# Attention and two feed-forward layers on one core: a chunk's last transpose tied to a product with 64 weight columns

## The chip, the cores and the metric

The kernel runs on one NeuronCore of a Trainium2 chip. The metric is the time of one execution on the device in microseconds (us), as a median of several runs. Five engines work side by side, each through its own list of instructions in order: TensorE (PE, matrix products and transposes; its weight loads show as PEld), VectorE (DVE), ScalarE (ACT), GpSimd (POOL) and SyncE (SP, which here only issues transfers). Products write to PSUM, eight banks of 128 x 512 numbers in float32; the other engines read them there.

## The reference

Attention over buckets, 2 batches x 8 heads x 768 tokens x 64 columns, then two feed-forward layers on 1536 tokens of 512 columns:

```python
q_bits = (einsum(q, proj) > 0); k_bits = (einsum(k, proj) > 0)   # 6 bits each
mask = q_bucket[:, :, :, None] == k_bucket[:, :, None, :]
scores = where(mask, q @ k.T / sqrt(64), -1e9)
attn = exp(scores - max); attn = attn / (sum(attn) + 1e-9)
x = (attn @ v)                         # -> 1536 x 512
h = x @ w_in;  x = (h * tanh(log1p(exp(h)))) @ w_out      # first layer, 2048 wide
h = x @ w_in2; x = (h - tanh(h)) @ w_out2                 # second layer
```

## The kernel before, in words

**Precision.** A number is kept as a high part (rounded to the PE's fast float32 form) and a low part (the rest). A product of two such numbers is made from high x high, high x low and low x high.

**Attention** goes through 8 pairs of heads. For a pair `g` each of the two heads `h` has two halves of 384 query tokens. A half takes three score tiles (`scores`, 128 tokens against 768 keys, four products, L507 and L508), into the only buffer `s` of two banks. DVE copies a tile to `p` with an upper clamp and takes its minimum on the way (L511, "clamp" below); ACT makes the exponentials and their sums (L533). The mask is part of the scores: the products in L508 carry the bits of the buckets beside the low parts of q and k. The bits come from a product with the planes (`piece`, L412 to L414, 64 weight columns), written to `z` (L395 on ACT, L397 on DVE), and from there by transfers into the stacks `c` and `d`; for the very first stack they are also written straight into `c` and `d`.

Then the half goes through 6 chunks of 128 keys (`chunk`): three PE transposes of `p` into a bank `pt` (L554), ACT's copy of it to the high part `ph` (L567), DVE's subtraction for the low part `pl` (L570), and a pair of products with the values `vt` (L578 with `ph`, L579 with `pl`). `vt` has 128 columns, 64 high and 64 low, so both products have 128 weight columns, and the output's two halves of 64 rows hold "times high" and "times low"; `gather` adds them into `u` (L586 on ACT, L589 on DVE). In three of a head's twelve chunks ("pooled") ACT copies to `f`, and POOL makes `ph` and `pl` from that (L319, L563). After the second head, `finish` makes the reciprocals of the sums (`rden`, L602 and L607 on DVE), spreads them (`wide`), transposes them on PE (L619) and multiplies (L626).

**Feed-forward.** The weights arrive as 64-bit words and are converted on DVE, ACT and POOL (`convert`, L711 to L740); the products are L756 to L758 and L815. The last block's results are copied to `osb` (two buffers) and sent out by SP (L865, L862).

**The order.** The whole program is first recorded as operations with a cost and a key (`op`). `Plan.order` then plays them through engine by engine with these costs, with the number of buffers and with a delay `LATE` between engines, takes at each step what can start first, and among equals the lowest key; in that order they are issued. Keys count in ticks of 1.16; a product's key lies `PV_LAG` ticks behind its chunk's. So other costs or other groupings change the order on all engines. PE takes its instructions strictly in the order made.

Of the kernel before, what the change touches and what calls it, by code (L numbers as in the profile page):

```python
# [39 lines left out]
N_A = 5  # L40
# [5 lines left out]
TAIL = 3  # L46
WARM = 7


G_BUFS, E_BUFS, GX_BUFS, F_BUFS = 3, 3, 2, 4  # L50
T_BUFS, O_BUFS, P_BUFS, U_BUFS = 3, 2, 6, 3

# [3 lines left out]
SPARE = 1  # L56
LATE = 0.25
LATS = 0.15
# [9 lines left out]
AHEAD = 8  # L68
PV_LAG = 4.0
PIECE = 2.5  # L70
# [4 lines left out]
V_REL = 14.0  # L75
Q_REL = 8.0
OUT_LAG = 13.0
RAW = 12.0
# [150 lines left out]
def tile_lsh_attention_moe(  # L229
# [55 lines left out]
    for name, m0, m1 in (("wb", N_A, N_A + N_B), ("wc", N_A + N_B, KF)):  # L285
        for tag in slots(m0, m1).split():
# [8 lines left out]
        memory("left", (  # L295
            ("const", "", 1), ("xy", "", 1), ("wa", slots(0, N_A), 1), ("osb", "osb", O_BUFS), ("t", "t", T_BUFS),
            ("g", "ph", G_BUFS), ("e", "pl", E_BUFS), ("f", "f", F_BUFS),
# [13 lines left out]

    zero = plan.pools["osb"].tile([P, XB], F32, tag="osb", name="zero")
    hot = plan.pools["osb"].tile([P, XB], F32R, tag="osb", name="hot")

# [86 lines left out]
    def piece(g, nm, half, key):  # L401

        if (g, "z") not in stacks:
            stacks[g, "z"] = buf("z", "z", [64, S], F32R)
        z, (th, tl) = stacks[g, "z"], stacks[g, nm]
        c = slice(half * HB, (half + 1) * HB)
        y = buf("ps_t", "pt", [P, 512])
        r0 = 0 if nm == "k" else 32

        def planes():  # L410
            o = y()[:64, :HB]
            nc.tensor.matmul(o, pjh, th()[:, c], start=True, stop=False)  # L412
# [3 lines left out]
        op("PE", 0.53, key + 0.3, planes, [(th, half), (tl, half)], [y])  # L416
# [123 lines left out]

    def chunk(g, h, half, c, ps, o, key):

# [7 lines left out]

        def transpose():
            for t in range(TB):
                pc = ps[t]().rearrange("p a b -> p (a b)")
                nc.tensor.transpose(pt()[:, t * P:(t + 1) * P], pc[:, c * P:(c + 1) * P], ident)  # L554

        op("PE", 0.41, key, transpose, ps, [pt])
        if pooled:
            pf = buf("f", "f", [P, XB])
            op("ACT", 0.38, key + 0.1, lambda: nc.scalar.copy(pf()[:, w], pt()[:, :HB]), [pt], [pf])
            op("POOL", 0.5, key + 0.2, lambda: pool_copy(ph()[:, w], pf()[:, w]), [pf], [ph], lat=LATG)  # L560
# [5 lines left out]
        else:  # L566
            op("ACT", 0.38, key + 0.1, lambda: nc.scalar.copy(ph()[:, w], pt()[:, :HB]), [pt], [ph])  # L567
            op(
# [3 lines left out]
                ),  # L572
                [pt, ph], [pl],
# [66 lines left out]
    for g in range(len(pairs)):  # L640
# [22 lines left out]
        for h in range(2):  # L663
            for half in range(2):
# [3 lines left out]
                ]  # L668
                o = buf("ps_t", "pt", [P, 512])
                for c in range(NT):  # L670
                    chunk(g, h, half, c, ps, o, at(NT * n + c))
                gather(h, o, us[half], at(NT * (n + 1)) + PV_LAG)
                if h == 1:
                    finish(g, half, us[half], at(NT * (n + 1)) + PV_LAG + 0.3)

# [146 lines left out]
    def feed_forward(which, j, first):  # L822
# [17 lines left out]
        for d, (a, n) in enumerate(acc):  # L840
# [13 lines left out]
            else:  # L854
                b, t = divmod(j * TX + d, NT)
                rows = out[b * S:(b + 1) * S, :].rearrange("(t p) d -> t p d", p=P)[t]
                osb = buf("osb", "osb", [P, DM])
                eng, cost, e = (("ACT", 0.48, nc.scalar.copy), ("DVE", 0.6, nc.vector.tensor_copy))[d % 2]
                if tail and d == KD - 1:
                    for i in range(2):  # L860
                        c = slice(i * hm, (i + 1) * hm)
                        op("ACT", 0.26, key, lambda osb=osb, a=a, n=n, c=c: nc.scalar.copy(osb()[:, c], a()[:, n, c]), [(a, n)], [(osb, i)])  # L862
                        dma(P * hm * 4, key, lambda rows=rows, c=c: rows[:, c], lambda osb=osb, c=c: osb()[:, c], [(osb, i)], [("out", j, d, i)])
                    continue
# [97 lines left out]
```

## Time and profile before

| what | value |
|---|---|
| median of 3 runs | 792.76 us (791.81 to 794.22) |
| profiled execution | 792.33 us, of which the span in the profile 790.6 us |
| PE busy | 769.4 us, 97% of the span |
| DVE, ACT, POOL busy | 489.3, 408.0, 302.1 us |
| attention | about 20 to 250 us |
| granted PE clock, mean | 0.997 |

The profile is of one execution. An idle time with an arrow is time in which the engine had nothing to do, and names what ended it; a PE instruction's length has a modelled end, so the distance between two starts says more than the length. The start of a product right behind a transpose is shown early, by the time that the transpose still takes; the start of the product after that one is true again.

### The profile page before, as it was taken

The numbers are of one execution on the slowest core, as the hardware profiler recorded it, in microseconds if no ns is written. First come the engines' busy times: TensorE is split into PE (matmuls) and PEld (weight loads), VectorE is DVE, ScalarE is ACT, GpSimd is POOL, SyncE is SP. The second block draws the span as 40 slices with busy tenths as digits, with TensorE's granted clock in tenths as the row PEclk, the third lists the DMA queues.
The fourth block names the chain that finished last, engine by engine and source line by source line (L and its number), as shares of the span: only waits on it lengthen the run. The fifth ranks groups of instructions, "written<-read, shape, count | busy, mean of one in ns | idle before, by whom it ended". The sixth has DMA issues, their size and how long they took to land.

```text
span 790.6 us, 10579 instructions
## 1 busy us (share of the span) xinstructions
PE 769.4 (97%) x3799; PEld 647.2 (82%) x3799; DVE 489.3 (62%) x792; ACT 408.0 (52%) x799; POOL 302.1 (38%) x308
## 2 busy tenths in 40 slices
PE   7999999999998899999999999999999999999997
PEld 5799898898887788887888888888887888888886
DVE  7888888898898998862111279889832322232221
ACT  6889899899888455443121345465522222222122
POOL 4676667667658766540000056555500000000000
PEclk9999999999999999999999999999999999999999
DMA  6574474563790460000000354530000100010001
GB/s 168 138 171 110 106 165 107 114 159 85 183 353 20 185 240 1 1 0 1 1 0 27 107 212 167 208 133 1 1 0 1 54 0 1 1 53 1 1 0 54
DMA packets 23009, 65.82 MB, mean 83 GB/s; under 512 B 3494, under 2 KB 4390, under 8 KB 22956
## 3 DMA queue, kind: packets, MB, share of 16 engines
q1 hardware_dynamic: 22524, 64.65, 27.5%
q8 instruction: 30, 0.49, 0.2%
q10 hardware_dynamic: 432, 0.49, 0.2%
q14 instruction: 23, 0.19, 0.1%
HBM read 43.09 MB, written 3.15 MB: 58 GB/s over the span
## 4 chain that ended last, share of the span: by engine, by line
PE 79%; DVE 12%; ACT 5%; issue 2%; DMA 1%; POOL 0%; ACTq 0%; DVEq 0%; POOLq 0%
PE s L815 17%; PE pt L815 16%; PE pt L758 11%; PE pt L756 11%; PE pt L757 11%; DVE p L511 4%; PE s L507 3%; PE pt L554 3%; PE s L508 3%; ACT p L533 2%; DVE pl L570 2%; PE pt L579 2%; PE pt L578 2%; DVE u L589 1%; DVE z L397 1%
## 5 line engine op out<-in xcount | busy, mean ns | idle before, releaser
L758 PE MATMUL pt<-xh,wi 128*128 128x512 f32 x384 | 151.1, 394 | 2.4 <-POOL wi L740 2.4
L756 PE MATMUL pt<-xh,wi 128*128 128x512 f32 x384 | 151.0, 393 | 0.0
L757 PE MATMUL pt<-xl,wi 128*128 128x512 f32 x384 | 150.7, 393 | 0.0
L794 DVE TENSOR_TENSOR pt<-pt,f 128x512 f32<-128x512 f32 x48 | 33.4, 697 | 118.1 <-ACT f L791 118.1
L784 DVE TENSOR_TENSOR pl<-f,ph 128x512 fp32r<-128x512 f32 x48 | 47.7, 996 | 88.3 <-ACT ph L781 88.1
L732 POOL TENSOR_TENSOR t<-t,wi 128x512 uint32<-128x512 uint32 x32 | 48.0, 1499 | 133.8 <-ACT wi L727 128.0
L533 ACT ACTIVATE p<-p,mn 128x768 f32<-128x768 f32 x96 | 90.3, 941 | 15.6 <-DVE p L511 13.3
L511 DVE TENSOR_SCALAR_CACHE_REDUCE p<-s 128x768 f32<-128x768 f32 x93 | 88.2, 948 | 12.7 <-PE s L508 12.0
L780 ACT ACTIVATE f<-pt 128x512 f32<-128x512 f32 x48 | 28.7, 598 | 129.8 <-PE pt L758 129.3
L791 ACT ACTIVATE f<-pt 128x512 f32<-128x512 f32 x48 | 28.7, 598 | 126.9 <-PE pt L758 126.6
L554 PE MATMUL pt<-cst,p 128*128 128x128 f32 x576 | 89.4, 272 | 1.6 <-ACT p L533 0.9
L758 PEld LDWEIGHTS pt<-xh,wi 128*128 128x128 f32 x384 | 72.1, 188 | 19.3 <-POOL wi L740 2.8
L756 PEld LDWEIGHTS pt<-xh,wi 128*128 128x128 f32 x384 | 72.2, 188 | 16.1
L757 PEld LDWEIGHTS pt<-xl,wi 128*128 128x128 f32 x384 | 72.1, 188 | 16.0
L554 PEld LDWEIGHTS pt<-cst,p 128*128 128x128 f32 x576 | 72.2, 140 | 8.8 <-ACT p L533 1.5
L570 DVE TENSOR_TENSOR pl<-pt,ph 128x384 fp32r<-128x384 f32 x146 | 76.2, 550 | 4.8 <-ACT ph L567 4.0
L507 PE MATMUL s<-b,a 128*128 128x384 f32 x186 | 69.1, 371 | 5.5 <-DVE p L511 5.0
L578 PE MATMUL pt<-ph,vt 128*128 128x384 f32 x192 | 72.7, 379 | 1.6 <-DVE pl L570 1.0
L567 ACT CAST ph<-pt 128x384 fp32r<-128x384 f32 x146 | 67.2, 476 | 8.9 <-PE pt L554 5.9
L579 PE MATMUL pt<-pl,vt 128*128 128x384 f32 x192 | 65.9, 343 | 1.4 <-DVE pl L570 1.3
L508 PE MATMUL s<-d,c 77*128 77x384 f32 (+1 forms) x186 | 63.7, 342 | 1.1 <-DVE d L397 1.0
L732 POOL TENSOR_TENSOR t<-t,wo 128x512 uint32<-128x512 uint32 x32 | 48.2, 1508 | 36.0 <-ACT wo L727 24.0
(109 smaller groups left out, 1546.6 us busy)
## 6 DMA issues: line engine op xcount, KB each, us to landing
wi<-in_moe_w_in_dram SPq DMA_DIRECT2D x32, 512.0 KB
wo<-in_moe_w_out_dram SPq DMA_DIRECT2D x32, 512.0 KB
b<-kh SPq DMA_DIRECT2D x30, 192.0 KB
v<-in_v_dram SPq DMA_DIRECT2D x8, 384.0 KB
a<-qh SPq DMA_DIRECT2D x15, 192.0 KB
a<-ql SPq DMA_DIRECT2D x15, 192.0 KB
d<-kl SPq DMA_DIRECT2D x15, 192.0 KB
c<-qh SPq DMA_DIRECT2D x15, 192.0 KB
```

Source lines behind the costliest of these rows:

```text
L507: nc.tensor.matmul(o, a()[:, tok], b_()[:, kc], start=True, stop=False)
L508: nc.tensor.matmul(o, c_()[used, tok], d_()[used, kc], start=False, stop=True)
L511: nc.vector.tensor_scalar(out=out, in0=in_, scalar1=MASKED, scalar2=None, op0=ALU.min, op1=ALU.min, accum_out=low)
L533: lambda: nc.scalar.activation(out=p(), in_=p(), func=AF.Exp, bias=mn(), scale=-1.0, accum_out=sm()[:, h, t:t + 1],),
L554: nc.tensor.transpose(pt()[:, t * P:(t + 1) * P], pc[:, c * P:(c + 1) * P], ident)
L570: lambda: nc.vector.tensor_tensor(out=pl()[:, w], in0=pt()[:, :HB], in1=ph()[:, w], op=ALU.subtract),
L578: nc.tensor.matmul(o()[:, :HB], vc, ph()[:, w], start=(c == 0), stop=False)
L732: lambda: nc.gpsimd.tensor_tensor(out=t(), in0=t(), in1=word(0), op=ALU.add),
L756: nc.tensor.matmul(h(), w()[:, 0, c], xh[kk][:, cols], start=(kk == 0), stop=False)
L757: nc.tensor.matmul(h(), w()[:, 0, c], xl[kk][:, cols], start=False, stop=False)
L758: nc.tensor.matmul(h(), w()[:, 1, c], xh[kk][:, cols], start=False, stop=(kk == KD - 1))
L815: nc.tensor.matmul(o, x, y, start=st and i == 0, stop=sp and i == 2)
```

## The change

Six edits go together.

1. In `chunk`, a new function `product` takes the place of the local one. A list `queue` holds the chunks whose product is still to come. From the fifth chunk on, a chunk first makes two transposes, and its third transpose is recorded as one operation together with the product of the chunk four before: third transpose, low product, high product. For a half's first chunk the high product comes first, ahead of the third transpose.
2. The low product has only the 64 columns of the high part of the values as weights; low times low is left out. `vt` has its high part first for both heads.
3. In the first pair, `z` is released from 12.5 on in the plan, and four filling products (`warm`) follow the planes of k's second half. The warm-up has 9 products, and `hot` is filled by one memset instead of a memset and a copy.
4. The costs that the plan counts for a chunk's PE work are others (0.33, 0.22 and 0.43), and `LATE` is 0.22.
5. Output rows are copied to buffers of the pool `f` (four) instead of `osb` (two).
6. The last tile's two halves are copied by ACT and DVE and sent by ACT's and SP's queue.

```diff
-WARM = 7
+WARM = 9
-LATE = 0.25
+LATE = 0.22
-PV_LAG = 4.0
+PV_LAG = 4
+Z_REL = 12.5
+FILL = 4
...
-        op(eng, cost, key + 0.4, lambda: bits(nm, z()[r, c], y(), r), [y], [(z, nm, half)])
+        op(eng, cost, key + 0.4, lambda: bits(nm, z()[r, c], y(), r), [y], [(z, nm, half)], release=0.0 if g else Z_REL)
+        if (g, nm, half) == (0, "k", 1):
+            o = buf("ps_t", "pt", [P, 512])
+
+            def warm():
+                for _ in range(FILL):
+                    nc.tensor.matmul(o()[:, :HB], hot[:, 0:P], hot[:, :HB], start=True, stop=True)
+
+            op("PE", 0.2 * FILL, key + 0.35, warm, [], [o], after=[first])
...
-        hi, lo = (slice(0, D), slice(D, 2 * D))[::1 if h == 0 else -1]
+        hi, lo = slice(0, D), slice(D, 2 * D)
...
+    def product(todo, late=None, key=0.0):
+        vt, c, ph, pl, o, done = todo
+        reads, writes = [(vt, 0), (vt, 1), ph, pl], [o]
+        if late:
+            reads += late[1]
+            writes += late[2]
+
+        def high():
+            nc.tensor.matmul(o()[:, :HB], vt()[:, c, :], ph()[:, :HB], start=(c == 0), stop=(c == NT - 1))
+
+        def emit():
+            if c == 0:
+                high()
+            if late:
+                late[0]()
+            nc.tensor.matmul(o()[:D, :HB], vt()[:, c, :D], pl()[:, :HB], start=False, stop=False)
+            if c:
+                high()
+
+        op("PE", 0.43 if late else 0.35, key, emit, reads, writes)
+        if done:
+            done()
...
-        op("PE", 0.41, key, transpose, ps, [pt])
+        if len(queue) < PV_LAG:
+            op("PE", 0.33, key, lambda: transpose(range(TB)), ps, [(pt, 0), (pt, 1)])
+        else:
+            op("PE", 0.22, key, lambda: transpose(range(TB - 1)), ps[:-1], [(pt, 0)])
+            product(queue.pop(0), (lambda: transpose((TB - 1,)), ps[-1:], [(pt, 1)]), key + 0.05)
...
-        def product():
-            vc = vt()[:, c, :]
-            nc.tensor.matmul(o()[:, :HB], vc, ph()[:, w], start=(c == 0), stop=False)
-            nc.tensor.matmul(o()[:, :HB], vc, pl()[:, w], start=False, stop=(c == NT - 1))
-
-        op("PE", 0.35, key + PV_LAG, product, [(vt, 0), (vt, 1), ph, pl], [o])
+        queue.append((vt, c, ph, pl, o, done))
...
-                osb = buf("osb", "osb", [P, DM])
+                osb = buf("f", "f", [P, DM])
...
-                        op("ACT", 0.26, key, lambda osb=osb, a=a, n=n, c=c: nc.scalar.copy(osb()[:, c], a()[:, n, c]), [(a, n)], [(osb, i)])
+                        eng, cost, e = (("ACT", 0.26, nc.scalar.copy), ("DVE", 0.34, nc.vector.tensor_copy))[i]
...
-    nc.vector.memset(zero, 0.0)
-    nc.vector.tensor_copy(hot, zero)
+    nc.vector.memset(hot.bitcast(F32), 0.0)
```

The order on DVE at the change from one pair of heads to the next, before. `p,mn<-s` is a clamp, `rden` the reciprocals of the sums of the pair's first half:

```order
L511 TENSOR_SCALAR p,mn<-s 128x768
L570 TENSOR_TENSOR pl<-pt,ph 128x384
L589 TENSOR_TENSOR u<-pt,f 64x384
L602 TENSOR_SCALAR rden<-sums 128x6
L607 RECIPROCAL rden<-rden 128x6
L511 TENSOR_SCALAR p,mn<-s 128x768
```

The same place on DVE now (the first row is again the clamp of the last tile that `rden` sums):

```order
L520 TENSOR_SCALAR p,mn<-s 128x768
L611 TENSOR_TENSOR pl<-pt,ph 128x384
L520 TENSOR_SCALAR p,mn<-s 128x768
L624 TENSOR_TENSOR u<-pt,f 64x384
L611 TENSOR_TENSOR pl<-pt,ph 128x384 x2
L520 TENSOR_SCALAR p,mn<-s 128x768
L611 TENSOR_TENSOR pl<-pt,ph 128x384
L637 TENSOR_SCALAR rden<-sums 128x6
L611 TENSOR_TENSOR pl<-pt,ph 128x384
L642 RECIPROCAL rden<-rden 128x6
L520 TENSOR_SCALAR p,mn<-s 128x768
```

`rden` has moved back past two clamps and three smaller operations, and a subtraction stands between it and its reciprocal.

The order on PE between two score tiles of the same stretch, before (L507 and L508 are scores, L554 transposes):

```order
L508 MATMUL s<-d,c 128x384
L578 MATMUL pt<-ph,vt 128x384
L579 MATMUL pt<-pl,vt 128x384
L554 MATMUL pt<-cst,p 128x128 x3
L578 MATMUL pt<-ph,vt 128x384
L579 MATMUL pt<-pl,vt 128x384
L554 MATMUL pt<-cst,p 128x128 x9
L507 MATMUL s<-b,a 128x384
```

PE now, between the two score tiles that have the least between them in a pair (L516 and L517 are scores, L590 transposes, L567 the low and L560 the high product):

```order
L517 MATMUL s<-d,c 128x384
L590 MATMUL pt<-cst,p 128x128 x2
L560 MATMUL pt<-ph,vt 128x384
L590 MATMUL pt<-cst,p 128x128
L567 MATMUL pt<-pl,vt 64x384
L590 MATMUL pt<-cst,p 128x128 x4
L516 MATMUL s<-b,a 128x384
```

Products stand alone or in pairs behind a transpose now, and the runs of nine transposes are gone from this stretch.

The order on DVE at the start, before: bits into `d` and `z` of the first stack, up to the first clamp.

```order
L397 TENSOR_SCALAR d<-pt,cst 13x384
L397 TENSOR_SCALAR z<-pt,cst 26x384
L463 COPY d<-kl 64x384
L397 TENSOR_SCALAR d<-pt,cst 13x384
L397 TENSOR_SCALAR z<-pt,cst 26x384
L378 SCALAR_TENSOR_TENSOR ql<-q,qh 128x384
L511 TENSOR_SCALAR p,mn<-s 128x768
```

DVE at the start now:

```order
L398 TENSOR_SCALAR d<-pt,cst 13x384
L472 COPY d<-kl 64x384
L398 TENSOR_SCALAR d<-pt,cst 13x384
L520 TENSOR_SCALAR p,mn<-s 128x768
L520 TENSOR_SCALAR p,mn_227<-pt 128x384
```

Both `z` and the low part of q's second half have moved behind the first clamps. On ACT the bits `c` of q's second half, which stood ahead of the first exponential, now stand behind the first three and one `z`.

## Rows read from the trace of the kernel before

**Rows 1.** Page, part 1: busy us, share of the span, instructions.

```profile
PE 769.4 (97%) x3799; PEld 647.2 (82%) x3799; DVE 489.3 (62%) x792; ACT 408.0 (52%) x799; POOL 302.1 (38%) x308
```

**Rows 2.** Stretches: length, busy PE, PEld, DVE, ACT, POOL, granted clock, DMA.

```profile
10.80:14.20 3.40, 3.26 (x10) 2.97 (x11) 3.34 (x11) 0.23 (x1) 0.75 (x2) 0.50 0.63 172
...
32.00:220.00 188.00, 182.83 (x1193) 169.72 (x1192) 167.73 (x364) 166.23 (x362) 129.22 (x167) 1.00 0.56 134
```

**Rows 3.** Waits of DVE, 32 to 220 us: us in total, times, longest.

```profile
DVE rden L602 <- ACT p L533: 7.1, 7, 1.0
```

**Rows 4.** Groups, 32 to 220 us: busy, mean ns, idle before, what ended it.

```profile
L507 PEld LDWEIGHTS s<-b,a 128*128 128x128 f32 x154 | 29.1, 189 | 9.9 <-DVE p L511 9.4
```

**Rows 5.** Timeline of PE: start, length, engine, line, idle before.

```profile
34.06 0.44 PE L507 MATMUL s<-b,a 128*128 128x384 f32 x1 [0.67 <-DVE p L511]
...
58.21 0.34 PE L508 MATMUL s<-d,c 77*128 77x384 f32 x1
...
61.50 1.14 PE L554 MATMUL pt<-cst,p 128*128 128x128 f32 x9
63.32 0.44 PE L507 MATMUL s<-b,a 128*128 128x384 f32 x1 [0.68 <-DVE p L511]
63.60 0.34 PE L508 MATMUL s<-d,c 77*128 77x384 f32 x1
```

**Rows 6.** Timeline of DVE, the same stretch.

```profile
58.58 0.96 DVE L511 TENSOR_SCALAR_CACHE_REDUCE p<-s 128x768 f32<-128x768 f32 x1 [0.34 <-PE s L508]
...
61.57 0.63 DVE L602 TENSOR_SCALAR rden<-sums 128x6 f32<-128x6 f32 x1 [1.01 <-ACT p L533]
...
62.34 0.92 DVE L511 TENSOR_SCALAR_CACHE_REDUCE p<-s 128x768 f32<-128x768 f32 x1
```

**Rows 7.** Timeline of ACT, the same stretch.

```profile
60.51 0.94 ACT L533 ACTIVATE p<-p,mn 128x768 f32<-128x768 f32 x1
```

**Rows 8.** Timeline of PE, transposes ahead of 64 and of 128 columns.

```profile
141.33 0.49 PE L554 MATMUL pt<-cst,p 128*128 128x128 f32 x3
141.58 0.42 PE L412 MATMUL pt<-kh,pjh 128*64 128x384 f32 x1
141.84 0.34 PE L413 MATMUL pt<-kh,pjl 128*64 128x384 f32 x1
...
142.53 0.49 PE L554 MATMUL pt<-cst,p 128*128 128x128 f32 x3
...
143.04 0.34 PE L579 MATMUL pt<-pl,vt 128*128 128x384 f32 x1
```

**Rows 9.** Groups of the whole span: weight loads of 128 and 64 columns.

```profile
L579 PEld LDWEIGHTS pt<-pl,vt 128*128 128x128 f32 x192 | 36.5, 190 | 3.5 <-DVE pl L570 2.1 <-POOL pl L563 1.1
...
L413 PEld LDWEIGHTS pt<-qh,pjl 128*64 128x64 f32 x16 | 2.3, 147 | 0.6
```

**Rows 10.** Timeline of PE, start.

```profile
10.94 0.69 PE L508 MATMUL s<-d,c 128*128 128x384 f32 x1 [0.98 <-DVE d L397]
```

**Rows 11.** Timeline of DVE, start.

```profile
10.82 0.66 DVE L397 TENSOR_SCALAR z<-pt,cst 26x384 fp32r<-26x384 f32 x1
...
11.87 0.94 DVE L511 TENSOR_SCALAR_CACHE_REDUCE p<-s 128x768 f32<-128x768 f32 x1
```

**Rows 12.** Timeline of ACT, start.

```profile
13.97 0.57 ACT L395 ACTIVATE c<-pt,cst 13x384 fp32r<-13x384 f32 x1 [3.59 <-PE pt L414]
14.57 0.94 ACT L533 ACTIVATE p<-p,mn 128x768 f32<-128x768 f32 x1
```

**Rows 13.** Timeline of POOL, the low part of the next pair's k.

```profile
73.09 1.01 POOL L388 TENSOR_TENSOR kl<-k,kh 128x384 fp32r<-128x384 f32 x1 [1.50 <-DMA d<-kl]
```

**Rows 14.** Timeline of PE, passage into the first feed-forward layer.

```profile
267.89 0.50 PE L758 MATMUL pt<-xh,wi 128*128 128x512 f32 x1 [2.41 <-POOL wi L740]
```

**Rows 15.** Timeline of PE and ACT, end.

```profile
785.92 0.39 PE L815 MATMUL pt<-wo,pl 128*128 128x512 f32 x1
787.12 0.65 ACT L862 COPY osb<-pt 128x256 f32<-128x256 f32 x2 [0.85 <-DMA out_dram<-osb]
```

More of the change, by code (lines that the diff above doesn't have):

```diff
@@ L46 @@
 TAIL = 3
-WARM = 7
+WARM = 9
 G_BUFS, E_BUFS, GX_BUFS, F_BUFS = 3, 3, 2, 4
-T_BUFS, O_BUFS, P_BUFS, U_BUFS = 3, 2, 6, 3
+T_BUFS, P_BUFS, U_BUFS = 3, 6, 3
 EPS = 0.005
 SPARE = 1
-LATE = 0.25
+LATE = 0.22
 LATS = 0.15
@@ L310, in tile_lsh_attention_moe @@
     xl = [xy_p.tile([P, B * S], F32R, name=f"xl{kk}") for kk in range(KD)]
-    zero = plan.pools["osb"].tile([P, XB], F32, tag="osb", name="zero")
-    hot = plan.pools["osb"].tile([P, XB], F32R, tag="osb", name="hot")
+    hot = const.tile([P, XB], F32R, name="hot")
     def x_tok(which, kk, t0, n):
@@ L414, in planes @@
             nc.tensor.matmul(o, pjh, tl()[:, c], start=False, stop=True)
-        op("PE", 0.53, key + 0.3, planes, [(th, half), (tl, half)], [y])
+        first = op("PE", 0.53, key + 0.3, planes, [(th, half), (tl, half)], [y])
         eng, cost = ("ACT", 0.55) if nm == "q" else ("DVE", 0.59)
@@ L539, in scores, with chunk @@
         return p
-    def chunk(g, h, half, c, ps, o, key):
+    def product(todo, late=None, key=0.0):
[17 more added lines that the diff above has]
+            done()
+    queue = []
+    def chunk(g, h, half, c, ps, o, key, done):
         vt = vts[g, h]
@@ L549, in chunk, with transpose @@
         w = slice(0, HB)
-        def transpose():
-            for t in range(TB):
+        def transpose(ts):
+            for t in ts:
                 pc = ps[t]().rearrange("p a b -> p (a b)")
                 nc.tensor.transpose(pt()[:, t * P:(t + 1) * P], pc[:, c * P:(c + 1) * P], ident)
-        op("PE", 0.41, key, transpose, ps, [pt])
+        if len(queue) < PV_LAG:
[3 more added lines that the diff above has]
+            product(queue.pop(0), (lambda: transpose((TB - 1,)), ps[-1:], [(pt, 1)]), key + 0.05)
+        both = [(pt, 0), (pt, 1)]
         if pooled:
             pf = buf("f", "f", [P, XB])
-            op("ACT", 0.38, key + 0.1, lambda: nc.scalar.copy(pf()[:, w], pt()[:, :HB]), [pt], [pf])
+            op("ACT", 0.38, key + 0.1, lambda: nc.scalar.copy(pf()[:, w], pt()[:, :HB]), both, [pf])
             op("POOL", 0.5, key + 0.2, lambda: pool_copy(ph()[:, w], pf()[:, w]), [pf], [ph], lat=LATG)
@@ L566, in chunk @@
         else:
-            op("ACT", 0.38, key + 0.1, lambda: nc.scalar.copy(ph()[:, w], pt()[:, :HB]), [pt], [ph])
+            op("ACT", 0.38, key + 0.1, lambda: nc.scalar.copy(ph()[:, w], pt()[:, :HB]), both, [ph])
             op(
@@ L572, in chunk @@
                 ),
-                [pt, ph], [pl],
+                [*both, ph], [pl],
             )
-        def product():
-            vc = vt()[:, c, :]
-            nc.tensor.matmul(o()[:, :HB], vc, ph()[:, w], start=(c == 0), stop=False)
-            nc.tensor.matmul(o()[:, :HB], vc, pl()[:, w], start=False, stop=(c == NT - 1))
-        op("PE", 0.35, key + PV_LAG, product, [(vt, 0), (vt, 1), ph, pl], [o])
+        queue.append((vt, c, ph, pl, o, done))
     def gather(h, o, u, key):
@@ L669, in tile_lsh_attention_moe, with done @@
                 o = buf("ps_t", "pt", [P, 512])
+                def done(g=g, h=h, half=half, o=o, u=us[half], key=at(NT * (n + 1)) + PV_LAG):
+                    gather(h, o, u, key)
+                    if h == 1:
+                        finish(g, half, u, key + 0.3)
                 for c in range(NT):
[L671 to L674, printed above, removed]
+                    chunk(g, h, half, c, ps, o, at(NT * n + c), done if c == NT - 1 else None)
+    for i, todo in enumerate(queue):
+        product(todo, None, at(n_items + i))
     wb_es = ExitStack()
@@ L861, in feed_forward @@
                         c = slice(i * hm, (i + 1) * hm)
-                        op("ACT", 0.26, key, lambda osb=osb, a=a, n=n, c=c: nc.scalar.copy(osb()[:, c], a()[:, n, c]), [(a, n)], [(osb, i)])
-                        dma(P * hm * 4, key, lambda rows=rows, c=c: rows[:, c], lambda osb=osb, c=c: osb()[:, c], [(osb, i)], [("out", j, d, i)])
+                        eng, cost, e = (("ACT", 0.26, nc.scalar.copy), ("DVE", 0.34, nc.vector.tensor_copy))[i]
+                        op(eng, cost, key, lambda osb=osb, a=a, n=n, c=c, e=e: e(osb()[:, c], a()[:, n, c]), [(a, n)], [(osb, i)])
+                        if i:
+                            dma(P * hm * 4, key, lambda rows=rows, c=c: rows[:, c], lambda osb=osb, c=c: osb()[:, c], [(osb, i)], [("out", j, d, i)])
+                        else:
+                            op(
+                                "ACT", 0.1, key + 0.1, lambda rows=rows, c=c, osb=osb: nc.scalar.dma_start(out=rows[:, c], in_=osb()[:, c]),
+                                [(osb, i)], [("out", j, d, i)], lat=3.0,
+                            )
                     continue
```

2 lines of the change are left out of this document (1 added, 1 removed).

## The prediction

> **What bounds the kernel now.** I read the page first: TensorE (PE) is busy 97% of 790.6 us [rows 1]. Then the table of stretches, since that share mixes stages. From 32 to 220 us (attention in its steady part) PE is busy 182.8 of 188 us, VectorE (DVE) 167.7, ScalarE (ACT) 166.2 [rows 2]: PE sets the pace, DVE and ACT have about 20 us to spare, and PE's "busy" has modelled ends, so its true idle time is more than 5 us. After its last long wait, at 267.89 us [rows 14], PE runs the feed-forward products back to back and the change leaves these alone, so I look at attention, the start, the passage into the first feed-forward layer, and the end.
>
> Next, who waits for whom. In the steady part DVE stands still 7.1 us in 7 waits at `rden`, for ACT's exponentials [rows 3]. PE's side is the weight load of the scores (L507): 9.4 us of idle time before it, ended by DVE's clamp (L511) [rows 4]. The timeline shows that the first wait makes the larger part of the second. The clamp of a score tile reads the one PSUM buffer `s`, so the next scores wait for it. At 61.57 DVE comes to `rden` after idling 1.01 us, because the exponential that it needs began only at 60.51 and takes 0.94 [rows 6, 7]; the clamp queued behind it starts at 62.34 instead of about 61.3; on PE the nine transposes from 61.50 are done at about 62.5 (0.11 each, see below), the scores start at 63.32 [rows 5]: 0.82 us lost. The second score product follows 0.28 later, where 0.175 is usual: 0.10 more, because its weight load too was held up. So 0.92 us a pair of heads, and it comes back every 29.26 us (34.06, 63.32 in [rows 5]), seven times as at `rden`: 6.5 of the 9.4 us. The rest, 2.9 us, are small waits where little PE work stands between two scores.
>
> **The change part by part.**
>
> *Transposes and 64 columns.* Per chunk PE did three transposes and two products with 128 weight columns; now the product of the low half of P has 64 (the term low times low goes). The moving side stays at 384 columns, so its own time stays: what can shrink is only what its weight load costs behind a transpose. The kernel already has such a place: three transposes, then the plane product with 64 columns (L412). From the first transpose to the product after it: 141.33 to 141.84, 0.51 us; with a 128-column product behind: 142.53 to 143.04, 0.51 us [rows 8]. Take off 0.175 for the product and a transpose is 0.11 in both. In the rows' steps of 0.01 nothing is gained; by the order 188 of the new low products stand right behind a transpose, so the bound is 188 x 0.01 = 1.9 us. I take 0. The number of transposes (576) and products (384) does not change, so splitting them costs no PE work by itself.
>
> The weight load itself is shorter, 147 ns against 190 [rows 9], and that is no contradiction: a load runs beside the product before it. The Trainium skill (TensorE: Matmul & The Clock Gate, section LDWEIGHTS (loading the stationary operand)) says that a load takes the number of columns divided by 1.2 GHz, hence half for 64. By that rule, taken as what ends last, the term would be an estimated 188 x 53 ns = 10 us instead of 0; the trace agrees that the load is shorter and not that it ends last here.
>
> If the 43 ns of [rows 9] did show behind a transpose, against [rows 8], the term would be 188 x 0.043 = 8 us; that is a rival below.
>
> *The new order.* Every product now stands exactly four chunks behind its transposes, and DVE's order changes with it. Before, a `pl` and a `u` stood between the clamp of the last tile that `rden` sums and `rden` itself; now two more clamps and three more small operations stand there. The two clamps alone are 1.9 us (0.96 each), against the 1.01 us that it waited [rows 6]. So this wait goes, 6.5 us on PE. What is late next: the scores, where the work between two of them is short. A clamp starts 0.37 us after the last score product's start (58.21 and 58.58 in [rows 5, 6]), and the next scores come 0.98 after the clamp's start (62.34 and 63.32); less the product's 0.175, PE needs about 1.2 us of other work between. By the order (0.11 for a transpose, 0.175 for a product) six of the twelve gaps in a pair had 1.35 to 1.38; now two have 1.35, one 1.22 and one 1.11, the others 1.53 or more. I count 0.3 us a pair for these, 2.1 us in seven pairs. Attention: 9.4 - 2.1 = 7.3 us less. Bounds: 9.4 (no wait left) and 0 (they only move).
>
> *The start.* DVE makes the score bits `d` before the bits `z` for later stacks: two `z` of 0.66 us leave the path [rows 11]. PE waits 0.98 us for `d` at 10.94 [rows 10], and the first clamp, at 11.87, can start about 1.2 us sooner. On ACT the first exponential stood behind the bits `c` of the second half of q: 13.97, then 14.57 [rows 12]; now three exponentials come first, so it can follow the clamp at about 11.7, 2.9 us sooner. But `c` then ends at about 11.7 + 3 x 0.93 + 0.6 + 0.6 = 15.7 instead of 14.5, and the second half's scores with it: 1.1 later. Both halves count about equally: I take 1.0 us gained, bounds 2.9 gained and 1.1 lost. The four filling products stand where PE waits anyway (0.98 us, some 0.6 shorter now, for 0.7 us of work); uncovered they would cost that 0.7. They may keep the clock up: from 10.8 to 14.2 us it was granted at 0.50, the level of 1.2 GHz [rows 2], after PE had stood idle from 9.96 on [rows 10]. At the full level that is at most 1.7 us of PE work, in a stretch that waits for ACT; it is inside the bound. The two warm-up products more begin sooner by one DVE copy and lie before PE's first operands are there; I cost them at nothing, uncovered at 2 x 0.69, the longest product of [rows 10].
>
> *The passage into the feed-forward.* Here DVE is the fuller engine, and PE has one long wait, 2.41 us at 267.89 for converted weights [rows 14]. The weights' conversions stand later in DVE's order than before and fewer feed-forward products fill attention's last chunks. I take 0, with 3 us gained (that wait gone) and 5 us lost (two waits of that kind more) as bounds.
>
> *The end.* The last product starts at 785.92 and is over at about 786.3; the last two copies begin at 787.12 after 0.85 us of waiting for an output transfer to free one of two buffers [rows 15]. Now there are four buffers: 0.85 less. The halves are copied on ACT and DVE side by side, not in a row, and leave by two queues: 0.3 less. What follows the copies, 790.6 - 787.77 = 2.8 us, stays. Together 1.1, bounds 0.5 and 1.3. The buffers come from the pool `f`, which the feed-forward's tanh also uses; a transfer holds one some 3 us, hidden by the 13 us that the plan lets the output products lag.
>
> **Sum**, against the profiled execution's 792.33 us (the runs' median is 0.4 above it): 792.33 - 7.3 - 1.0 - 1.1 = 782.9; I say 783.
>
> **Rivals.**
> 1. *The waits only move.* The `rden` wait goes, but the gaps of 1.11 and 1.22 us, or the products tied to a transpose, stop PE as long. For it: every clamp still passes one buffer, and DVE is at 89% (167.7 of 188, [rows 2]). Against: DVE's work between two clamps is nearly always less than PE's between two scores in the new order. Then only start and end remain: 792.3 - 2.1 = 790.2.
> 2. *The weight load decides.* [rows 9] speak for it, [rows 8] against: 782.9 - 8 = 775.
> 3. *The passage gives it back:* 782.9 + 5 = 788.
> 4. *Slower: the tied group.* The low product stands between a transpose and the high product, and everything on PE stands behind it. The low half of a pooled chunk comes from GpSimd (POOL), and once a pair POOL's order puts `kl` ahead of it; `kl` waited 1.50 us for a transfer and takes 1.01 [rows 13]. It decides once that half comes over 4.3 us (four chunks of PE work by the order) after its transposes. At the full 2.5 us for seven pairs: 782.9 + 17.5 = 800. Against: before, `kl` stood there too, and no pooled `pl` stopped PE for long.
> That the change doesn't do what it says is rival 2's mirror: the 64 columns then bring nothing, which is my forecast.
>
> **How the numbers follow.** Forecast 0.64 (its own range 779 to 787), rival 1 0.16, rival 2 0.05, rival 3 0.08, rival 4 0.07. The range 776.5 to 790.5 leaves out rival 4, rival 2 and the edges of the others. A difference under 0.3% (2.4 us) can't be told from none: rival 1 lies on that edge. Faster 0.64 + 0.05 + 0.08 + half of rival 1, less a little: 0.83; same 0.10; slower 0.07.
>
> **What would show it.** Right: no wait at `rden` on DVE, the idle time before the scores' weight load down from 9.4 to 2 or 3 us, a pair of heads 1 us shorter than 29.26, the last copies right behind the last product, 0.51 us again for three transposes and the next product. Wrong: 0.46 or less there (rival 2), waits of products for `pl` (rival 4), waits of scores as long as before (rival 1), longer waits for weights between 230 and 270 us (rival 3).

## The result, and the profile after

The changed kernel takes 780.94 us (median of 4 runs, 780.87 to 781.23) and the kernel before, beside it on the same chip, 793.24 us (791.81 to 794.22). The ratio is 0.985, with a 95% interval of 0.984 to 0.987. The profiled execution took 780.97 us, of which its span is 779.2. The prediction was 783.0 with a range of 776.5 to 790.5. First, page part 1 and the stretches of [rows 2], columns as there.

```profile
PE 767.8 (99%) x3805; PEld 642.4 (82%) x3805; DVE 480.7 (62%) x792; ACT 404.9 (52%) x798; POOL 298.0 (38%) x308
```

```profile
10.80:14.20 3.40, 2.30 (x11) 1.28 (x11) 3.37 (x11) 2.27 (x5) 0.64 (x2) 1.00 0.91 198
32.00:220.00 188.00, 187.38 (x1238) 172.70 (x1237) 173.34 (x376) 168.89 (x375) 129.34 (x172) 1.00 0.59 140
```

PE does the same work in less time: in steady attention it is busy 187.4 of 188 us, where it was 182.8, and issues 1238 products and transposes instead of 1193. At the start the granted clock stays at 1.00 where it was 0.50. Next the waits of DVE from 32 to 220 us, and the groups of [rows 4]:

```profile
DVE p L520 <- PE s L517: 8.3, 20, 0.9
DVE p L520 <- PE pt L590: 2.6, 6, 0.4
DVE pl L611 <- ACT ph L608: 1.4, 6, 0.2
```

```profile
L516 PEld LDWEIGHTS s<-b,a 128*128 128x128 f32 x160 | 30.2, 189 | 4.4 <-DVE p L520 4.2
L567 PEld LDWEIGHTS pt<-pl,vt 128*64 128x64 f32 x161 | 22.0, 136 | 2.0
```

The 7.1 us at `rden` [rows 3] are gone from DVE's list, and what it waits for now is mostly PE, as it should where PE sets the pace. The idle time ahead of the scores' weight load fell from 9.4 to 4.2 us. The load of the low product is shorter (136 ns for 64 columns, 190 for 128 in [rows 9]). Timelines of DVE and ACT show where `rden` stands now (L637):

```profile
84.04 0.96 DVE L520 TENSOR_SCALAR_CACHE_REDUCE p<-s 128x768 f32<-128x768 f32 x1 [0.41 <-PE s L517]
86.22 0.96 DVE L520 TENSOR_SCALAR_CACHE_REDUCE p<-s 128x768 f32<-128x768 f32 x1 [0.44 <-PE pt L590]
88.50 0.94 DVE L520 TENSOR_SCALAR_CACHE_REDUCE p<-s 128x768 f32<-128x768 f32 x1
...
89.84 0.34 DVE L637 TENSOR_SCALAR rden<-sums 128x6 f32<-128x6 f32 x1
```

```profile
85.46 0.95 ACT L542 ACTIVATE p<-p,mn 128x768 f32<-128x768 f32 x1
```

The exponential that `rden` needs (of the tile clamped at 84.04) is over at 86.4, and DVE comes for it at 89.84, two clamps later. On PE a pair of heads now takes 28.16 us (63.78 to 91.94, against 29.26 in [rows 5]), and three transposes with a 64-column product behind them take 0.50 us from the first to the product after (83.84 to 84.34):

```profile
63.78 0.44 PE L516 MATMUL s<-b,a 128*128 128x384 f32 x1
...
83.84 0.49 PE L590 MATMUL pt<-cst,p 128*128 128x128 f32 x3
84.08 0.42 PE L567 MATMUL pt<-pl,vt 128*64 128x384 f32 x1
84.34 0.34 PE L560 MATMUL pt<-ph,vt 128*128 128x384 f32 x1
...
91.94 0.45 PE L516 MATMUL s<-b,a 128*128 128x384 f32 x1
```

The two profiled executions took 792.33 and 780.97 us. Where these 11.4 us came from is read by laying the same instruction of both traces side by side (times in us from the span's start, from the timelines of PE):

| instruction | before | after | gained so far |
|---|---|---|---|
| first scores of the second pair | 38.52 | 35.65 | 2.9 |
| last product of attention | 256.49 | 245.84 | 10.65 |
| last product of all | 785.92 | 775.29 | 10.63 |
| end of the span | 790.55 | 779.18 | 11.4 |

So the start, up to the second pair, gave 2.9, attention from there on 7.8, the passage and the feed-forward layers nothing, the end 0.7. Of the 7.8, six pairs gave 6.9 (214.27 to 204.53 at the first scores of the last pair); the last pair, which shares its place with feed-forward products, gave 0.9.

### The profile page after: what moved, and what is told of

Read it like the earlier page. It is cut to its first block, busy times and chain, and to the rows that moved or that the text cites. A ratio compares the mean times of both kernels' runs of the same rounds, so it can differ in the third digit from the quotient of the medians.

```text
span 779.2 us, 10565 instructions
## 1 busy us (share of the span) xinstructions
PE 767.8 (99%) x3805; PEld 642.4 (82%) x3805; DVE 480.7 (62%) x792; ACT 404.9 (52%) x798; POOL 298.0 (38%) x308
## 4 chain that ended last, share of the span: by engine, by line
PE 92%; DVE 5%; issue 1%; ACT 1%; DMA 0%; POOL 0%; ACTq 0%; DVEq 0%
PE s L855 17%; PE pt L855 16%; PE pt L798 11%; PE pt L796 11%; PE pt L797 11%; PE pt L590 7%; PE s L516 4%; PE pt L567 4%; PE pt L560 4%; PE s L517 4%; DVE p L520 1%; DVE pl L611 1%; DVE t L751 1%; PE pt L654 1%; PE pt L415 1%
## 5 line engine op out<-in xcount | busy, mean ns | idle before, releaser
L590 PE MATMUL pt<-cst,p 128*128 128x128 f32 x576 | 105.9, 274 | 2.2 <-ACT p L542 1.0
L824 DVE TENSOR_TENSOR pl<-f,ph 128x512 fp32r<-128x512 f32 x48 | 41.6, 866 | 100.3 <-ACT ph L821 100.3
L590 PEld LDWEIGHTS pt<-cst,p 128*128 128x128 f32 x576 | 75.1, 140 | 11.7 <-ACT p L542 2.1
L567 PE MATMUL pt<-pl,vt 128*64 128x384 f32 x192 | 80.2, 418 | 0.2 <-DVE pl L611 0.2
L608 ACT CAST ph<-pt 128x384 fp32r<-128x384 f32 x146 | 67.5, 475 | 13.8 <-PE pt L560 13.5
L516 PE MATMUL s<-b,a 128*128 128x384 f32 x186 | 67.1, 361 | 0.8 <-DVE p L520 0.7
L560 PE MATMUL pt<-ph,vt 128*128 128x384 f32 x192 | 66.5, 348 | 0.3 <-DVE z L398 0.3
L517 PE MATMUL s<-d,c 77*128 77x384 f32 (+1 forms) x186 | 63.4, 341 | 0.1
L855 PE MATMUL s<-ph,wo 128*128 128x512 f32 x192 | 60.5, 395 | 1.2 <-DVE wo L780 0.8
```

The costliest lines, as they stand in the source:

```text
L516: nc.tensor.matmul(o, a()[:, tok], b_()[:, kc], start=True, stop=False)
L517: nc.tensor.matmul(o, c_()[used, tok], d_()[used, kc], start=False, stop=True)
L560: nc.tensor.matmul(o()[:, :HB], vt()[:, c, :], ph()[:, :HB], start=(c == 0), stop=(c == NT - 1))
L567: nc.tensor.matmul(o()[:D, :HB], vt()[:, c, :D], pl()[:, :HB], start=False, stop=False)
L855: nc.tensor.matmul(o, x, y, start=st and i == 0, stop=sp and i == 2)
```

## The experiments

Theory: attention gained because the sum of the denominators (`rden`) no longer stands on DVE where it must wait for an exponential; the 64 columns gave next to nothing; the start gained by the late bits of `z`. Rivals: the 64 columns, the filling products and the clock, the tie of a transpose to a product. The times of before beside these runs were 791.8 to 792.7 us (medians). "The mark" is the first score of the second pair, 35.65 us in the changed kernel.

**The low product with 128 columns** (in the changed kernel):

```
- matmul(o()[:D, :HB], vt()[:, c, :D], pl()...)
+ matmul(o()[:, :HB],  vt()[:, c, :],  pl()...)
```

> The changed kernel with one edit: the low product multiplies by all 128 weight columns again, as before the change, in the same place and the same order of instructions (its upper 64 columns add the low-times-low term, which the changed kernel leaves out). Theory (the gain of attention is the order on VectorE, not the 64 columns): the load for 128 columns stands behind a transpose of about 110 ns that covers nearly all of it; start to next start of low and high product was 264 ns before and 258 ns after, so some 190 products times 6 ns give 1.1 us: 782.1 us, between 781.4 and 783.0, and a pair of heads of 28.3 us instead of 28.15. Rival (the 64 columns give the gain of attention): a pair of heads goes back to 29.2 us and the time to 788 to 789 us.

Measured: 781.60 us, ratio to before 0.986 (0.985 to 0.988): 0.7 us above the changed kernel. The weight load is back to 189 ns (the group's row) and PE's timeline shows the same step, 84.19 to 84.70, 0.51 us:

```profile
L567 PEld LDWEIGHTS pt<-pl,vt 128*128 128x128 f32 x161 | 30.5, 189 | 1.9
```

```profile
84.19 0.49 PE L590 MATMUL pt<-cst,p 128*128 128x128 f32 x3
84.44 0.42 PE L567 MATMUL pt<-pl,vt 128*128 128x384 f32 x1
84.70 0.34 PE L560 MATMUL pt<-ph,vt 128*128 128x384 f32 x1
```

Over 134 such places from 32 to 220 us the low product holds PE for 260 ns with 128 columns and 258 with 64. A pair takes 28.17 us (28.15 to 28.16 with 64 columns). Of the 0.57 us by which the span is longer, 0.33 was there at the mark (and at the first scores, before any low product), and 0.24 arose behind it. The 64 columns are worth 0.2 us of 11.4. The Trainium skill (TensorE: Matmul & The Clock Gate, section LDWEIGHTS (loading the stationary operand)) makes the load proportional to its columns. The trace agrees on the difference, 189 less 136 = 53 ns for 64 columns, but not on the proportion (136 of 189 ns is not half), and it shows that the load does not end last here.

**`rden` later, alone** (in the kernel before):

```
  op("DVE", 0.08, key, rden = sm + 1e-9, ...,
+    after=[clamps[g, 1, 1, 1]] if half == 0 else [])
  # finish() of the first half is called after the second half's chunks
```

> The kernel before with one edit of order: the sum of the denominators of the first half of a pair (rden) stands on VectorE behind the second clamp of the next half instead of in front of the first; nothing else of the change is in it (128 columns, old start, old end). Theory (the order is the gain of attention): the waits of VectorE at rden go, the idle time of TensorE ahead of the weight load of a score falls from 9.4 us to 3 or less, a pair of heads takes 28.2 to 28.4 us instead of 29.26, and the time is 792.8 less seven pairs at 0.9: 786.5 us, between 785.5 and 788. Rival (64 columns): nothing changes, 792.5 to 793.3. A third way (another wait takes its place, since ScalarE and VectorE are nearly full): 790 to 792.

Measured: 784.97 us, ratio 0.990 (0.989 to 0.992): 7.7 us less than before, by one small instruction, with what hangs on it, moved behind two clamps. In steady attention (stretch, then group):

```profile
32.00:220.00 188.00, 187.30 (x1238) 175.44 (x1237) 172.72 (x378) 171.99 (x376) 133.94 (x173) 1.00 0.60 147
```

```profile
L508 PEld LDWEIGHTS s<-b,a 128*128 128x128 f32 x160 | 30.3, 189 | 3.4 <-DVE p L512 2.3
```

1238 instructions of PE, as many as in the changed kernel, and no wait at `rden`; a pair takes 28.22 us, 1.03 less than before. The order alone gives nearly all of attention's 1.1 us a pair. Of the 6.9 us by which the span is shorter, 6.1 lie in attention and 0.6 at the end, where this kernel has the old code (see the end, below).

**`rden` early again** (in the changed kernel):

```
+ early[g] = denom(g, 0, ...)         # rden recorded with the first half's scores
+ after=[early[g]] on the clamp of tile 0, half 1, head 1
```

> The changed kernel with one edit of order: the sum of the denominators of the first half of a pair is put on VectorE back in front of the first clamp of the next half, as it stood before the change; the 64 columns, the tied transposes, the start and the end stay. Theory (order): the wait at rden comes back with about 1.0 us a pair on VectorE and 0.8 to 0.9 us of it on TensorE; seven pairs give 6 us: 787 us, between 785 and 788.5, a pair of heads of 29.0 us. Rival (64 columns): 781 us, within 0.7.

Measured: 789.77 us, ratio 0.996 (0.995 to 0.997): 8.8 us lost, more than the 6 expected. The wait is back (DVE's waits, then PE's groups, 32 to 220 us), but PE loses in two places:

```profile
DVE rden L636 <- ACT p L544: 5.3, 6, 0.9
```

```profile
L592 PEld LDWEIGHTS pt<-cst,p 128*128 128x128 f32 x461 | 59.3, 140 | 11.5 <-ACT p L544 3.8 <-ACT f L602 1.7
L517 PEld LDWEIGHTS s<-b,a 128*128 128x128 f32 x154 | 29.1, 189 | 6.9 <-DVE p L521 6.1
```

The scores wait as before, and the transposes now wait for exponentials too (3.8 us; none was listed in the changed kernel). A pair takes 29.40 us, 1.25 more. Of the span's 8.8 us, 1.8 are there at the mark (the first pair has such a wait too), 7.5 come in six pairs, and 0.5 is given back behind them. The direction and the place are as the theory has them; its price was taken from the kernel before, where no wait of the transposes for exponentials was listed in steady attention.

**Without the tie** (in the changed kernel; the 64 columns stay):

```
- op("PE", 0.22, key, transpose 0 and 1 ...)
- product(queue.pop(0), (transpose 2 ...), key + 0.05)
+ op("PE", 0.33, key, transpose 0, 1 and 2 ...)
+ product(queue.pop(0), None, key + 0.05)     # planned at 0.32
```

> The changed kernel without the tie: the three transposes are one step of the plan again and the product is a step of its own (planned at 0.33 and 0.32 us), with the 64 columns and the order low, high kept. The planner then puts rden in front of the first clamp of the next half again, behind only one subtraction, and puts two products in a row in some places, where a weight load of 64 columns stands behind a product instead of a transpose. Theory (order): most of the wait at rden comes back, a pair of heads takes 28.8 to 29.2 us and the time is 785 to 788 us, likeliest 786.5. Rival (64 columns): the loads are the same as in the changed kernel, 781 us, within 0.7; by this rival a product in a row with another would even gain more.

Measured: 782.70 us, ratio 0.987 (0.986 to 0.989). Both expectations failed. `rden` stands in front of the first clamp only in every second pair, and there it waits little (DVE's waits, then its timeline at one of these):

```profile
DVE rden L637 <- ACT p L542: 1.1, 3, 0.4
```

```profile
57.34 0.38 DVE L637 TENSOR_SCALAR rden<-sums 128x6 f32<-128x6 f32 x1 [0.36 <-ACT p L542]
57.64 0.94 DVE L520 TENSOR_SCALAR_CACHE_REDUCE p<-s 128x768 f32<-128x768 f32 x1
```

From mark to mark pairs now take 29.2 and 27.3 us by turns, as the products of 27 and of 21 chunks stand in them; two take 56.4 us, 28.2 each. The mark comes 0.4 us sooner than with the tie and attention ends 0.3 sooner. What matters is therefore not the place of `rden` in DVE's row, but whether ACT is done when DVE comes there. The tie brings attention nothing by itself; which other part of the change moves `rden` (where `finish` is recorded, the costs, `LATE`) was not tried one by one. The 1.8 us were lost elsewhere: counted by feed-forward products, PE is 2.0 us ahead of the changed kernel up to 326 us and 1.7 behind at 348. In between, in the first feed-forward layer, the other order let products wait for ACT's and DVE's copies (PE's timeline):

```profile
330.07 0.73 PE L855 MATMUL s<-ph,wo 128*128 128x512 f32 x2 [0.53 <-ACT ph L821]
331.30 0.50 PE L855 MATMUL s<-pl,wo 128*128 128x512 f32 x1 [0.51 <-DVE pl L824]
337.23 0.73 PE L855 MATMUL s<-ph,wo 128*128 128x512 f32 x2 [0.54 <-ACT ph L821]
```

**No filling products** (`FILL = 4` to `0`):

> The changed kernel without the four filling products at the start (L430); nothing else differs up to the end of attention. Theory (they keep the granted clock): as in the kernel before, where TensorE stood idle ahead of the first scores, the granted clock falls to 0.50 somewhere between 10 and 15 us for some 3 us, TensorE's work there takes up to twice as long, and the first scores of the second group of tiles (the mark at 20.88 us in the changed kernel) come 0.5 to 1.7 us later: 781.4 to 782.6 us, likeliest 782. Rival (the two more warming products or the shorter start did it): the clock stays at 1.00, the four products were 0.9 us of idle time put to use, and the time is 780.7 to 781.1.

Measured: 780.95 us, ratio 0.985 (0.984 to 0.987), the changed kernel's time; the mark is at 35.66. The theory fell: from 10.8 to 14.2 us the clock is granted at 1.00 without them.

```profile
10.80:14.20 3.40, 2.31 (x11) 1.30 (x11) 3.37 (x11) 2.26 (x5) 0.54 (x2) 1.00 0.93 206
```

**Bits of `z` early** (`Z_REL = 12.5` to `0.0`):

> The changed kernel with the bits of z of the first pair planned as soon as they can be, as before the change, instead of from 12.5 us on. Theory (the start gains by the late bits): the copies of bits stand again ahead of the first clamps and exponentials on VectorE and ScalarE, 0.55 us each for four of them; the first exponential goes from 11.46 us back to between 12.5 and 14.5 us and the scores of the next pair (35.65 us in the changed kernel) come 1 to 2 us later: 782 to 783 us. Rival (the start gains by the clock alone): the first exponential moves by less than 0.6 us and the time by less than 0.5 us.

Measured: 783.82 us, ratio 0.989 (0.987 to 0.990). The mark moves from 35.65 to 37.62, 1.97 later, as expected. ACT's first exponential starts at 12.86 instead of 11.46, behind the bits `c`:

```profile
12.26 0.57 ACT L396 ACTIVATE c<-pt,cst 13x384 fp32r<-13x384 f32 x1 [2.33 <-PE pt L415]
12.86 0.94 ACT L542 ACTIVATE p<-p,mn 128x768 f32<-128x768 f32 x1
```

1.2 us of it are there at the next head's first scores (22.09 instead of 20.88). The rest goes with the clock, which fell at 21.8 us with the filling products in place, after PE had waited 0.79 us at 18.93 for ACT and 0.53 at 21.16 for DVE; at 0.50, the level of 1.2 GHz, a score product takes 0.52 us instead of 0.34 (stretches, then PE's timeline). The four executions agree: at a mean granted clock of 0.998 they took 784.11 and 784.08 us, at 0.999 783.56, at 1.000 783.36.

```profile
21.00:22.00 1.00, 0.81 (x3) 0.39 (x4) 0.26 (x2) 1.00 (x4) 1.00 (x2) 0.92 0.89 200
22.00:23.00 1.00, 1.00 (x4) 1.00 (x4) 1.00 (x2) 1.00 (x3) 1.00 (x2) 0.50 0.06 12
```

```profile
18.93 0.42 PE L560 MATMUL pt<-ph,vt 128*128 128x384 f32 x1 [0.79 <-ACT ph L608]
...
21.16 0.39 PE L413 MATMUL pt<-kh,pjh 128*64 128x384 f32 x1 [0.53 <-DVE pl L611]
...
22.43 0.52 PE L517 MATMUL s<-d,c 77*128 77x384 f32 x1
```

The total is 2.9 us (3.1 in the profiled executions) and not 2: another order at the start also changes the passage, which here gained 2.9 against the changed kernel up to the last product of attention and gave back 4.1 behind it.

**The last half in a tile of its own:**

```
  for i in range(2):      # the two halves of the last output rows
+     if i: osb = buf("t", "t", [P, DM])
```

> The changed kernel with VectorE's half of the last output rows written to a tile of its own; the copy, its size and its queue stay. In the changed kernel this copy began at 776.17 us, when ScalarE's copy of the other half had ended, 0.88 us behind the last product's start. Theory (the shared output tile makes it wait): it now begins with ScalarE's copy, 0.4 us earlier, and the span behind the last product's start shrinks from 3.89 us to about 3.5: 780.5 us. Rival (the shared accumulator makes it wait): the copy still begins where ScalarE's ends, and the span behind the last product stays at 3.89 within 0.1: 780.9 us. A third way (the copies run side by side, but ScalarE's queue is the one that ends last): the copy is earlier and the end is not.

Measured: 780.99 us, ratio 0.985 (0.984 to 0.987): nothing. Timelines of ACT and DVE, of the changed kernel and of this one:

```profile
775.77 0.37 ACT L903 COPY f<-pt 128x256 f32<-128x256 f32 x1 [1.48 <-PE pt L855]
776.17 0.35 ACTq L908 DMA_DIRECT2D out_dram<-f  x1
776.17 0.42 DVE L903 COPY f<-pt 128x256 f32<-128x256 f32 x1 [2.58 <-ACT f L903]
```

```profile
775.85 0.37 ACT L905 COPY f<-pt 128x256 f32<-128x256 f32 x1 [1.47 <-PE pt L855]
...
776.25 0.42 DVE L905 COPY t<-pt 128x256 f32<-128x256 f32 x1 [2.58 <-ACT f L905]
```

With separate outputs DVE's copy still begins when ACT's has ended, so it is the accumulator that they share: the program makes the second reader wait for the first. The Trainium skill (PSUM — Partial Sum Buffer, section PSUM bank collisions raise a hardware error) says that the compiler adds a dependency between two engines that touch one bank and quadrant, two readers included; this trace agrees, with 0.40 us from copy to copy. Here the wait goes further than one bank: the two banks of the tile `s`, whose last products began by 771.86 us, are also copied one after the other (ACT and DVE, changed kernel):

```profile
772.28 0.59 ACT L912 COPY f<-s 128x512 f32<-128x512 f32 x1 [2.87 <-PE s L855]
772.90 0.69 DVE L912 COPY f<-s 128x512 f32<-128x512 f32 x1 [2.77 <-ACT f L912]
```

I overlooked this when I took the halves to be copied side by side.

**Two edits on the kernel before:** `rden` later as above, and

```
+ op(..., bits of z, ..., release=0.0 if g else 12.5)
```

> The kernel before with two edits: rden behind the second clamp of the next half (alone 784.97 us), and the bits of z of the first pair planned from 12.5 us on; 128 columns, no tie, seven warming products, no filling products, the old end. Theory (order of attention and late bits are all that matters but 0.7 us of the end): the late bits, taken back in the changed kernel, cost 1.97 us of its start, so the time is 783.0 us, and the scores of the second pair come near 36 us; the passage may move it by 2 us either way, so 781.5 to 785. Rival (the warming and filling products carry the start): the granted clock falls to 0.50 at the start as in the kernel before, and the start gains under 1 us: 784 to 785.

Measured: 784.07 us, ratio 0.990 (0.988 to 0.991). The mark is at 36.49, 1.67 sooner than with `rden` alone. The time does not show this: it is 0.9 below that of `rden` alone, but the runs of before beside it were 0.8 faster too, so the two ratios are the same, and both expectations allow it. Nor are the 1.67 us due to the bits' place alone, since in the trace of `rden` alone the clock was at 0.50 twice at the start (11.7 to 15.1 and 21.9 to 25.3 us). What speaks against the rival is the clock, which stays up here with seven warming products and no filling ones:

```profile
10.80:14.20 3.40, 2.29 (x11) 1.25 (x9) 3.35 (x12) 2.29 (x5) 0.23 (x1) 1.00 0.94 195
```

So with the late bits the clock holds at the start without the warming and filling products. Against the changed kernel 2.8 us of span are missing: 0.8 at the mark, 0.5 over six pairs, 1.3 in the last pair and the passage, 0.2 at the end.

**Three tries at a faster kernel.** The version without the tie, with the outer products planned 12 us (13 in the kernel) behind the hidden layer and the tile of its own:

> A try at a faster kernel: the version without the tie (its pair of heads took 28.03 us against 28.15 of the changed kernel, and it was 0.3 us ahead at the last product of attention, but lost 2.8 us between 329 and 482 us, where ScalarE's copies of a hidden layer waited for buffers that TensorE freed late), with the outer products planned 12 instead of 13 us behind the hidden layer, and with VectorE's own tile for the last half. If the loss hangs on how late the outer products are planned: 782.7 less 2 and less 0.3, 780.0 to 780.6. If it doesn't: 782.2 to 782.8.

Measured: 781.04 us, ratio 0.985 (0.984 to 0.987): 1.7 us of the loss came back, and it ties with the changed kernel. The changed kernel with later bits, 13.5 and 15.0:

> A try at a faster kernel: the changed kernel with the bits of z released at 13.5 instead of 12.5 us of the plan; on ScalarE the bits of the stack of the first head (c) then stand ahead of those of z, which stood 0.6 us ahead of them. If the exponentials of the second half start earlier by that much, the scores of the second pair come 0.5 us before 35.65 us and the time is 780.4 us, give or take 1.5 us for the passage, which another order at the start reshuffles; if the copies of z, which the next head's stack needs, come too late, the start loses 0.5 to 1 us: 781.5.

> The same try with 15.0 us: on VectorE two clamps of the second half now stand ahead of the bits of z as well. If the later bits still help: the scores of the second pair come 0.5 to 1.2 us before 35.65 us, time 779.8 to 780.5; if the stack of the next head waits for them, its first scores (20.88 us in the changed kernel) come later than 21.5 us and the time is 781.5 to 783.

Measured: 782.14 us, ratio 0.987 (0.986 to 0.989), and 785.04, ratio 0.991 (0.989 to 0.993). With 13.5 the next head's scores come 0.3 sooner, but the mark 0.4 later; why was not traced. Its two executions at a granted clock of 1.000 took 781.27 and 781.47 us, the two at 0.997 782.81 and 783.07. With 15.0 the next head's scores come at 24.10 instead of 20.88 and the mark 1.9 later, another 2.7 us are lost behind attention's last product, and at 16.4 us the clock falls, after PE had waited 0.62, 0.17 and 0.67 us one after the other (PE's timeline, then stretches):

```profile
14.11 0.33 PE L590 MATMUL pt<-cst,p 128*128 128x128 f32 x1 [0.62 <-ACT p L542]
14.60 0.44 PE L516 MATMUL pt<-b,a 128*128 128x384 f32 x1 [0.17 <-DVE a L472]
15.72 0.41 PE L517 MATMUL pt<-d,c 128*128 128x384 f32 x1 [0.67 <-ACT c L396]
```

```profile
16.00:18.00 2.00, 2.00 (x10) 1.90 (x9) 1.45 (x3) 0.64 (x2) 2.00 (x3) 0.60 0.55 118
18.00:20.00 2.00, 2.00 (x10) 1.71 (x9) 1.97 (x7) 1.53 (x4) 2.00 (x4) 0.55 0.61 171
```

None beats the changed kernel: bits too early hold up the first exponentials, and bits as late as 15.0 the next head's stack.

## Why the prediction was right, and where its terms were off

| term | predicted | measured |
|---|---|---|
| 64 columns | 0 (bound 1.9) | 0.2 gained |
| order of attention | -7.3 | -7.8 from the second pair on, the 64 columns in it |
| start | -1.0 (-2.9 to +1.1) | -2.9 up to the second pair |
| passage | 0 (-3 to +5) | 0.0 |
| end | -1.1 (0.5 to 1.3) | -0.7 |
| sum | -9.4 | -11.4 |

**The order: right in place, and near in size partly by luck.** The wait at `rden` was the place: its removal alone gives 1.03 us a pair, against 0.92 worked out from one gap of the timeline. But the stretches of the table cut this term in two, for the first of the seven waits lies ahead of the mark (DVE, before; PE's idle time behind it is the 0.67 us at 34.06 in [rows 5]):

```profile
32.31 0.63 DVE L602 TENSOR_SCALAR rden<-sums 128x6 f32<-128x6 f32 x1 [1.01 <-ACT p L533]
```

At the prediction's price of 0.9 us that wait belongs to the order and not to the start; by this estimate the order gave 8.7 and the start 2.0. The order was thus mis-sized by 1.4 us, of which the last pair's 0.9 was not in the sum at all. In the steady pairs two misses offset each other: I counted 2.1 us of waits left ahead of the scores, and 4.2 are left; yet a pair became 1.10 us shorter (29.25 to 28.15), while this idle time fell only from 1.46 to 0.63 us a pair (188 us hold 6.4 pairs before and 6.7 now). The other 0.27 us a pair is not in that view, and its cause stays open. Rival 1, that the waits only move, is refuted by the shorter pair.

**The 64 columns: right.** The step of 0.51 us in [rows 8] told it before any run: the lengths of the load in [rows 9] would have given rival 2's 8 us, the step gave 0, the run 0.2. Rival 2 is refuted.

**The start: mis-sized too.** It gave about 2.0 us without the first pair's wait, where I had 1.0; taking back the late bits alone cost 1.97. I set a gain of 2.9 for the first half of the queries against a loss of 1.1 for the second, whose bits now stand behind the exponentials, and took about the middle. The loss did not come. ACT made `c` at 15.53 (13.97 in [rows 12]), but the first half's transposes and products, which came earlier, filled PE meanwhile, and the next head's scores began at 20.88 instead of 22.93. The clock, which I had put inside the bound, is part of it: with early bits it fell at 10.8 us in the kernel before and at 21.8 in the changed one, with the bits at 12.5 it stayed at 1.00 in the traces. For the filling products, which I had thought might keep it up, the runs show no effect. The two edits on the kernel before bring the mark from 38.52 to 36.49; what brings the last 0.8 us to 35.65 is not told apart.

**The passage: right as a sum.** The wait of 2.41 us [rows 14] went, and shorter ones took its place, the longest 0.79 us at 256.29. In the experiments the passage gave or took up to 4 us as the order changed; that it came out at zero is luck as much as insight, and the bounds of -3 and +5 were the honest part.

**The end: one step failed.** The wait for an output buffer went: the first of the two copies begins 0.48 us behind the last product's start instead of 1.20, so 0.72 was gained where I had 0.85 ([rows 15]). The 0.3 for copying the halves side by side did not come, because both read one accumulator: the copies take 0.82 us instead of 0.65. What follows them, forecast as unchanged, is 0.19 shorter. Nor is the wait a fixed price: in the two runs with the old end and a later `rden` it was 0.29 and 0.35 us (ACT, two edits), and the span behind the last product's start 4.07 and 4.12 us instead of 4.63. Beside these, the new end with its 3.89 is worth about 0.2.

```profile
778.57 0.65 ACT L866 COPY osb<-pt 128x256 f32<-128x256 f32 x2 [0.35 <-DMA out_dram<-osb]
```

Rival 4, the tied group waiting for `pl`, did not show: no product waited for POOL in steady attention.

## What to carry to other kernels

Where one engine's row of instructions holds an operation that needs the newest result of a second engine, everything behind it waits; moving it behind work that is ready cost nothing here and was worth some 60% of this change (6.9 of 11.4 us of span). A shorter weight load counts only where it ends last: compare the step from one product to the next in a place that already has the shorter load before counting columns. A planner's order is touched by every edit, so read a change stage by stage at the same instruction; here an edit at the start moved the passage by up to 4 us.

## What was not expected of the hardware

The granted clock fell to 0.50 behind waits on PE that were each below 1 us, at different places: at 10.8 us in the kernel before (during the 0.98 us ahead of the product at 10.94, [rows 10]), at 21.8 with early bits, and at 16.4 and again at 238 (behind 0.56 and 0.63 us) with the bits at 15.0. Other waits passed without a fall: 0.63 us at 14.04 in the changed kernel, three of 0.54 to 0.73 between 8 and 15 us with early bits, 1.28 at 238.76 without the tie. What decides is not shown by these runs. In steady attention of the changed kernel, where about two in five of PE's instructions are float32 transposes, the clock stayed at 1.00 throughout, and a transpose took 0.11 us from start to start; at 0.50 it took 0.21 (at 17.5 and 19.1 us with the bits at 15.0). Two engines that read different columns of one accumulator did so one after the other, 0.40 us apart.
